# Attention and a two-layer network in one kernel: turning q and k of nineteen quads on TensorE instead of by a transposing DMA

## The chip, the core and the metric

The kernel runs on one core of a Trainium2 chip. The metric is the device time of one execution, in microseconds (us). A core has a matrix engine (TensorE, PE in the profile; its weight loads are listed apart as PEld), VectorE (DVE), ScalarE (ACT), GpSimd (POOL) and a queue engine that only issues transfers (SyncE, SP). PSUM, where PE writes, has eight banks here, numbered 0 to 7. Each engine works through its own instructions in order.

## What is computed

```python
q, k, v                     # (8, 12, 448, 64): batch, heads, positions, head width
scores = scale * q @ k.T    # for each batch and head
attn   = maximum(scores, 0) ** 2 / 448
x      = attn @ v           # gathered to (3584, 768)
h      = x @ w_in           # (3584, 2048)
g      = maximum(h, 0) + alpha * minimum(h, 0)
out    = g @ w_out          # (3584, 768)
```

The score of a query and a key sums over the head width of 64, so PE needs q and k with the 64 columns of a head on the partitions and the positions along a row. They arrive the other way round, with positions on the partitions. "Turning" below means that step.

## The kernel before

**Tiling.** The 12 heads of a batch are taken four at a time, which gives 3 groups for each of 8 batches: 24 "quads", numbered 0 to 23. A quad has 7 chunks of keys. Matrix operands are bf16.

**The steps of a quad.** `load_qk` and `load_v` issue loads on POOL's queue into tiles of shape 128 x 896 (`raw`, three buffers each for q and k; `v`, six). q and k are turned into one tile `T` (four buffers). `score_mm` (L209) makes the scores of one chunk in a pair of PSUM banks, `relu` (L218 on ACT, L220 on DVE) and `square` (L231 on DVE, L229 on ACT) follow, and `attnv` (L241) multiplies with v over all 7 chunks and writes the quad's part of `xT`. When a batch has its three quads, `f1_mm` (L275) makes the first layer in 16 units of 6 matmuls, each followed by `f1_out` (L281 on ACT, then L282 on DVE); the second layer is either `f2` (L300) or a seven-product scheme (`Pair`, L335, with sums on DVE at L331 and L340).

**Two ways of turning.** Quads 0 to 4 go through `turn_pe` (L176 to L186). For each of q and k it takes a PSUM bank and issues 14 transposes on PE (7 position groups times 2 head halves, L183), each with 64 columns of the raw tile as weights and the 128-column identity streaming past; the two halves of a position group write partitions 0 to 63 and 64 to 127 of the bank. Then one copy (L186) brings the 128 x 896 bank to `T`. Quads 5 to 23 go through `turn_dma` (L188 to L199): two copies on ACT or DVE (L195) rearrange q and k into one tile (`perm`, a single buffer, or for quads 5, 7 and 8 a stretch of `w_mix`), and a transposing DMA on SP's queue (L197) writes `T`. After it, `land` (L418) makes POOL copy one element of `T`, so that POOL's queue stands still until the transfer has landed; the loads of later quads are issued behind it.

**What sets the order.** The order is written out by hand in the strings at L506 to L518, one word for each step, and each engine gets its instructions in that order. The words that matter here are `d6D` (turn quad 6, copies on DVE), `l6` (`land`), `n` (`prepare`: turn the next quad, then load q and k of the quad two further and v of the next), `c` (score chunks), `v` (`attnv`), `f`, `h`, `e`, `E` (first layer, in one go or in parts with a bank held) and `p1` to `p7`, `r1` to `r7` (second layer). `FIRST_PAIR`, `EACH`, `ONE_PAIR` and `LAST` are the plans of one batch each; `EACH` is run three times. The turn of a quad stands well ahead of its first chunk.

**Banks.** `take_bank` gives the bank that was taken longest ago; once `paired` is set it prefers the partner of the bank taken last. `take_pair` gives the pair of neighbours longest unused, `hold` withdraws a bank until it is given back. A matmul into a bank waits until the previous contents have been read.

Of the kernel before, what the change touches and what calls it, by code (L numbers as in the profile page):

```python
# [11 lines left out]
BF16 = mybir.dt.bfloat16  # L12
# [4 lines left out]
NJ = 7  # L17
# [3 lines left out]
def kernel(  # L21
# [10 lines left out]
    nc = tc.nc  # L32
    B, H, S, D = q.shape
# [11 lines left out]
    singles = ctx.enter_context(tc.tile_pool(name="singles", bufs=1))  # L45
    raw_pool = ctx.enter_context(tc.tile_pool(name="raw", bufs=3))
    v_pool = ctx.enter_context(tc.tile_pool(name="v", bufs=6))
    perm_pool = ctx.enter_context(tc.tile_pool(name="perm", bufs=1))
    T_pool = ctx.enter_context(tc.tile_pool(name="T", bufs=4))
    rl_pool = ctx.enter_context(tc.tile_pool(name="rl", bufs=6))  # L50
    at_pool = ctx.enter_context(tc.tile_pool(name="at", bufs=10))
# [11 lines left out]
    w_mix = [singles.tile([128, KH, NH], BF16, name=f"w_mix{i}") for i in range(4)]  # L63
# [3 lines left out]
    landed = singles.tile([1, 1], BF16)  # L67
# [17 lines left out]
    def hold():  # L85
        i = one()
        taken[i] = 10**9
        return i
# [14 lines left out]
    def take_bank():  # L103
        i = one()
        take(i, 1)
        return psum[:, i]


    raw, vraw = {}, {}

    def load_qk(n, names="qk"):
        b, g = divmod(n, NG)
        for name in names:
            src = q if name == "q" else k
            t = raw_pool.tile([128, 2, NJ, D], BF16, tag=name, name=f"{name}raw")
            flat = src[b].rearrange("(m two) (pp j) d -> (two pp) m (j d)", two=2, j=NJ)
            nc.gpsimd.dma_start(out=t.rearrange("p m j d -> p m (j d)"), in_=flat[:, 2 * g:2 * g + 2])
            raw[(n, name)] = t

    def load_v(n):  # L120
        b, g = divmod(n, NG)
        t = v_pool.tile([128, 2, NJ, D], BF16, tag="v", name="vraw")
        flat = v[b].rearrange("(m two) (pp j) d -> (two pp) m (j d)", two=2, j=NJ)
        nc.gpsimd.dma_start(out=t.rearrange("p m j d -> p m (j d)"), in_=flat[:, 2 * g:2 * g + 2])
        vraw[n] = t
# [28 lines left out]
    for lo, hi, eng in ((0, 4, nc.sync), (4, NJ, nc.scalar)):  # L154
        t = o_pool.tile([128, 2, (hi - lo) * D], F32, tag="o", name=f"qfirst{lo}")
# [18 lines left out]
    T = {}  # L174

    def turn_pe(n, parts=(("q", 0, NJ, "D"), ("k", 0, NJ, "D"))):  # L176
        if n not in T:
            T[n] = T_pool.tile([128, 2, NJ, 128], BF16, tag="T", name="T")
        for name, lo, hi, eng in parts:
            ps = take_bank().bitcast(BF16)  # L180
            for j in range(lo, hi):
                for s in range(2):
                    nc.tensor.transpose(ps[64 * s:64 * s + 64, 128 * j:128 * j + 128], raw[(n, name)][:, s, j], ident)  # L183
            dst = T[n][:, "qk".index(name), lo:hi].rearrange("p j c -> p (j c)")
            copy = nc.vector.tensor_copy if eng == "D" else nc.scalar.copy
            copy(dst, ps[:, 128 * lo:128 * hi])  # L186

    def turn_dma(n, eng="A"):  # L188
        if n in (5, 7, 8):
            w = w_mix[2 + n % 2].rearrange("p k c -> p (k c)")[:, :4 * NJ * D]  # L190
            p = w.rearrange("p (a j s d) -> p a j s d", a=2, j=NJ, s=2)
        else:
            p = perm_pool.tile([128, 2, NJ, 2, D], BF16, tag="perm", name="perm")
        for i, name in enumerate("qk"):
            (nc.vector.tensor_copy if eng == "D" else nc.scalar.copy)(p[:, i], raw.pop((n, name)).rearrange("p s j d -> p j s d"))  # L195
        t = T_pool.tile([128, 2, NJ, 128], BF16, tag="T", name="T")
        nc.sync.dma_start_transpose(out=t.rearrange("p a j c -> p (a j) c"),  # L197
                                    in_=p.rearrange("p a j s d -> p (a j s d)"))
        T[n] = t  # L199


    att, xT = {}, {}
# [58 lines left out]
    def chunk(eng):  # L261
        if stream:
            n, j = stream.pop(0)
            late.append((n, j, relu(score_mm(n, j), eng)))

    def sq(i, eng):
        if i < len(late):
            square(*late.pop(i), eng)
# [4 lines left out]
    def f1_mm(ps, b, ff, ks):  # L273
        for km in ks:
            nc.tensor.matmul(ps, w_in_sb[:, km // 2, km % 2, bass.ts(ff, 128)],  # L275
                             xT[b][:, km // 2, km % 2, :],
                             start=(km == 0), stop=(km == KM - 1))

    def f1_out(ps, b, ff):
        neg = neg_pool.tile([128, S], F32, tag="neg", name="neg")  # L280
        nc.scalar.activation(neg, ps, ACTF.Relu, scale=-1.0)  # L281
        nc.vector.scalar_tensor_tensor(gT[:, ff, (b % 2) * S:(b % 2) * S + S],  # L282
                                       neg, beta_sb[:, ff:ff + 1], ps, ALU.mult, ALU.add)
# [121 lines left out]
        copy = nc.vector.tensor_copy if eng == "D" else nc.scalar.copy  # L405
        copy(raw[(0, "q")][:, :, lo:hi].rearrange("p m j d -> p m (j d)"), qfirst[lo][:, :, :D * (hi - lo)])

    def prepare(n, eng="A"):
        if n < NQ:
            turn_dma(n, eng)  # L410
            land(n)
        if n + 2 < NQ:
            load_qk(n + 2)
        if n + 1 < NQ:
            load_v(n + 1)

    def land(n):
        nc.gpsimd.tensor_copy(landed, T[n][:1, 0, 0, :1])  # L418

    class Walk:  # L420

# [11 lines left out]
        def step(self, w):  # L433
            c, rest = w[0], w[1:]
            if c == "c":
                for eng in rest:
                    chunk(eng)
            elif c == "s":
                sq(int(rest[:-1] or 0), rest[-1])
            elif c == "v":  # L440
                if turn["v"] < NQ:
                    attnv(turn["v"], rest or "AD")
                    turn["v"] += 1
            elif c == "f":
                b, ff, ps, _ = self.unit(self.b, self.ff)
                f1_mm(ps, b, ff, range(KM))
                f1_out(ps, b, ff)
            elif c == "m":
                self.open = self.unit(self.b, self.ff)
                f1_mm(self.open[2], *self.open[:2], range(KM))  # L450
            elif c == "o":
                f1_out(self.open[2], *self.open[:2])
            elif c == "e":
                for i in range(self.parts, self.parts + int(rest)):
                    ff, km = divmod(i, 4)
                    if km == 0:
                        self.held.append(self.unit(self.b, self.ff, hold()))
                    f1_mm(self.held[ff][2], self.b, ff, (km,))
                self.parts += int(rest)
            elif c == "h":  # L460
                self.held.append(self.unit(self.b, self.ff, hold()))
                f1_mm(self.held[-1][2], *self.held[-1][:2], range(4))
            elif c == "E":
                b, ff, ps, bank = self.held.pop(0)
                f1_mm(ps, b, ff, range(4, KM))
                f1_out(ps, b, ff)
                take(bank, 1)
            elif c == "B":
                self.b, self.ff = self.b + 1, 0
            elif c in "pr":  # L470
                if rest[0] in "abcd":
                    getattr(self, c).mix("abcd".index(rest[0]) + 1)
                else:
                    getattr(getattr(self, c), "p" + rest)()
            elif c == "w":
                i, half = int(rest[0]), int(rest[1])
                weight_mix(i, 4 * half, 4 * half + 4)
            elif c == "g":
                f2(self.b // 2, int(rest[0]), int(rest[1]))
            elif c == "n":  # L480
                prepare(self.quad, rest or "A")
                self.quad += 1
            elif c == "x":
                cast0(int(rest[0]), int(rest[1]), rest[2])
            elif c == "t":
                turn_pe(int(rest[0]), ((rest[1], int(rest[2]), int(rest[3]), rest[4]),))
            elif c == "d":
                turn_dma(int(rest[:-1]), rest[-1])
            elif c == "l":
                land(int(rest))  # L490
            elif c == "L":
                n = [int(x) for x in rest[1:].split(",")]
                {"q": load_qk, "v": load_v, "i": load_w_in, "o": load_w_out}[rest[0]](*n)
            elif c == "i":
                warm(int(rest))
            elif c == "y":
                bank = min(range(8), key=lambda i: (taken[i], i))
                for _ in range(int(rest)):
                    nc.tensor.matmul(psum[:, bank, :128], idle, idle, start=True, stop=True)
            elif c == "z":  # L500
                two_queues.append(1)
            elif c == "b":
                nc.vector.tensor_scalar(beta_sb, alpha_sb, -1.0, 1.0, ALU.mult, ALU.add)
# [48 lines left out]
```

## Time and profile before

| | us |
|---|---|
| median of the runs (372.81 to 373.34) | 373.07 |
| the profiled execution, whole time | 373.07 |
| its span, first to last instruction | 371.3 |
| outside the span | 1.8 |
| score matmuls, L209, 672, busy | 45.9 |
| attention-times-v matmuls, L241, 672, busy | 36.6 |
| first layer, L275, 768, busy | 150.4 |
| relu on ACT, L218, 128, busy | 111.2 |
| gate on DVE, L282, 128, busy | 85.3 |

The granted TensorE clock is 1.000 of full speed over the span. The slices of the profile have PE at 9 tenths or more from the third slice to the last but one, DVE and ACT between 4 and 9 for most of the span, and the 16 DMA engines at 8 or 9 tenths for the first 13 slices (about 120 us), then between 8 and 0. "Busy" is the time in which an engine has an instruction in flight; matmuls overlap each other, so the busy times of groups of matmuls are unions and not sums. The chain of waits follows the work that ended last back to the start; its rows are start, duration, engine, line and number of instructions.

### The profile page before, as it was taken

How to read it: one execution, taken by the hardware profiler on the slowest of the kernel's cores; microseconds unless marked ns; L12 is line 12 of the kernel's file. 1: busy time of each engine (PE TensorE's matmuls, PEld its weight loads, DVE VectorE, ACT ScalarE, POOL GpSimd, SP SyncE). 2: the span in 40 equal slices, each digit the busy share in tenths (PEclk: the TensorE clock that was granted, in tenths of full speed). 3: DMA queues.
4: the chain of work that ended last, by engine and by line, in shares of the span. 5: the costliest groups of instructions: out<-in, count | busy, mean ns of one | idle time of the engine just before them, and what ended most of it. 6: DMA issues, size and time to landing. Idle time of an engine off the chain costs nothing.

```text
span 371.3 us, 7894 instructions
## 1 busy us (share of the span) xinstructions
PE 363.6 (98%) x3105; PEld 197.5 (53%) x3105; DVE 278.0 (75%) x445; ACT 274.7 (74%) x406; POOL 71.7 (19%) x120
## 2 busy tenths in 40 slices
PE   8799999999999999999999999999999999999995
PEld 6454564444554565545555455554555455555563
DVE  3989988885968989566887768888749667856653
ACT  5998676877997678885997859967699866964400
POOL 8566150304211222022020220202200000000000
PEclk9999999999999999999999999999999999999999
DMA  9999989999999868455882659727646201220024
GB/s 143 188 203 202 199 135 191 153 160 167 180 171 150 123 96 163 92 89 90 160 144 64 99 80 168 144 56 121 111 89 134 49 2 43 65 65 0 0 64 108
DMA packets 73557, 43.29 MB, mean 117 GB/s; under 512 B 40368, under 2 KB 73008, under 8 KB 73520
## 3 DMA queue, kind: packets, MB, share of 16 engines
q0 software_dynamic: 27136, 22.58, 42.0%
q1 hardware_dynamic: 45712, 19.61, 25.9%
q10 hardware_dynamic: 672, 0.59, 0.5%
q8 instruction: 24, 0.39, 0.4%
q14 instruction: 13, 0.11, 0.1%
HBM read 45.62 MB, written 11.01 MB: 153 GB/s over the span
## 4 chain that ended last, share of the span: by engine, by line
PE 94%; DVE 2%; ACT 2%; issue 1%; ACTq 0%
PE psum L275 38%; PE psum L335 30%; PE psum L241 9%; PE psum L209 9%; PE psum L300 6%; PE psum L183 1%; PE psum L165 1%; DVE gT L282 1%; ACT rl L218 1%; ACT xT L253 1%; ACT neg L281 1%; DVE w_mix L195 1%; DVE T L186 0%; DVE at L231 0%; DVE osb L340 0%
## 5 line engine op out<-in xcount | busy, mean ns | idle before, releaser
L275 PE MATMUL psum<-xT,w_in_sb 128*128 128x448 bf16 x768 | 150.4, 353 | 0.2 <-DVE gT L282 0.2
L282 DVE SCALAR_TENSOR_TENSOR gT<-neg,beta_sb,psum 128x448 bf16<-128x448 f32 x128 | 85.3, 679 | 43.4 <-ACT neg L281 42.1
L218 ACT ACTIVATE rl<-psum 128x896 bf16<-128x896 f32 x128 | 111.2, 925 | 6.7 <-PE psum L209 4.7
L275 PEld LDWEIGHTS <-w_in_sb 128*128 128x128 bf16 x768 | 73.4, 98 | 73.0 <-issue 6.8
L281 ACT ACTIVATE neg<-psum 128x448 f32<-128x448 f32 x128 | 68.5, 547 | 41.0 <-PE psum L275 32.7
L231 DVE TENSOR_TENSOR at<-rl 128x896 bf16<-128x896 bf16 x105 | 62.2, 620 | 0.5 <-ACT rl L218 0.2
L229 ACT ACTIVATE at<-rl 128x896 bf16<-128x896 bf16 x63 | 58.6, 952 | 0.3
L335 PEld LDWEIGHTS <-S 128*128 128x128 bf16 x384 | 36.7, 98 | 28.4 <-issue 5.3
L335 PE MATMUL psum<-w_mix,S 128*128 128x384 bf16 x288 | 49.8, 326 | 0.2
L220 DVE TENSOR_SCALAR rl<-psum 128x896 bf16<-128x896 f32 x40 | 43.2, 1086 | 8.7 <-PE psum L209 8.1
L209 PE MATMUL psum<-T 64*64 64x448 bf16 x672 | 45.9, 357 | 2.0 <-DVE T L186 1.0
L418 POOL COPY landed<-T 1x1 bf16<-1x1 bf16 x18 | 3.3, 181 | 206.1 <-DMA T<-perm 182.9
L335 PEld LDWEIGHTS <-gT 128*128 128x128 bf16 x296 | 28.3, 98 | 20.2 <-issue 1.8
L241 PE MATMUL psum<-at,vraw 64*64 64x448 bf16 x672 | 36.6, 350 | 0.0
L335 PE MATMUL psum<-w_out_sb,gT 128*128 128x384 bf16 x192 | 34.0, 326 | 0.0
L340 DVE TENSOR_TENSOR osb<-psum,u 128x384 f32<-128x384 f32 (+2 forms) x37 | 20.2, 547 | 12.6 <-PE psum L335 8.2
L209 PEld LDWEIGHTS <-T 64*64 64x64 bf16 x672 | 17.4, 105 | 22.7 <-issue 14.8
L241 PEld LDWEIGHTS <-vraw 64*64 64x64 bf16 x672 | 21.2, 106 | 11.9 <-issue 2.9
L300 PE MATMUL psum<-w_out_sb,gT 128*128 128x256 bf16 (+1 forms) x128 | 22.0, 326 | 0.1
L255 DVE TENSOR_SCALAR xT<-psum 128x448 bf16<-128x448 f32 x24 | 14.9, 622 | 8.9 <-PE psum L241 8.3
L253 ACT ACTIVATE xT<-psum 128x448 bf16<-128x448 f32 x24 | 13.3, 556 | 9.1 <-PE psum L241 8.7
L356 ACT COPY osb<-psum 128x384 f32<-128x384 f32 x12 | 5.8, 480 | 17.4 <-PE psum L335 17.4
(45 smaller groups left out, 242.0 us busy)
## 6 DMA issues: line engine op xcount, KB each, us to landing
out_dram<-osb SPq DMA_DIRECT2D x91, 96.0 KB, 2.2
vraw<-in_v_dram POOLq DMA_DIRECT2D x24, 224.0 KB, 6.5
qraw<-in_q_dram POOLq DMA_DIRECT2D x23, 224.0 KB, 4.1
kraw<-in_k_dram POOLq DMA_DIRECT2D x23, 224.0 KB, 5.3
w_in_sb<-in_moe_w_in_dram POOLq DMA_DIRECT2D x16, 192.0 KB, 8.0
w_out_sb<-in_moe_w_out_dram POOLq DMA_DIRECT2D x4, 512.0 KB, 9.5
w_out_sb<-in_moe_w_out_dram POOLq DMA_DIRECT2D x4, 256.0 KB, 8.8
out_dram<-osb SPq DMA_DIRECT2D x8, 128.0 KB, 3.2
```

Of the source, the lines that this page charges most:

```text
L209: nc.tensor.matmul(ps[64 * c:64 * c + 64, r, :S], t[64 * r:64 * r + 64, 1, j, 64 * c:64 * c + 64], t[64 * r:64 * r + 64, 0, :, 64 * c:64 * ...
L218: nc.scalar.activation(rl, ps[:, :, :S], ACTF.Relu)
L220: nc.vector.tensor_scalar(rl, ps[:, :, :S], 0.0, None, ALU.max)
L229: nc.scalar.activation(a, rl, ACTF.Square)
L231: nc.vector.tensor_tensor(a, rl, rl, ALU.mult)
L241: nc.tensor.matmul(ps[64 * s:64 * s + 64, r, :S], vv[64 * r:64 * r + 64, s, j, :], a[64 * r:64 * r + 64, s], start=(j == 0), stop=(j == NJ ...
L275: nc.tensor.matmul(ps, w_in_sb[:, km // 2, km % 2, bass.ts(ff, 128)], xT[b][:, km // 2, km % 2, :], start=(km == 0), stop=(km == KM - 1))
L281: nc.scalar.activation(neg, ps, ACTF.Relu, scale=-1.0)
L282: nc.vector.scalar_tensor_tensor(gT[:, ff, (b % 2) * S:(b % 2) * S + S], neg, beta_sb[:, ff:ff + 1], ps, ALU.mult, ALU.add)
L300: nc.tensor.matmul(ps, gT[:, ff, bass.ts(c, 128)], w_out_sb[:, ff, first_col + lo:first_col + hi], start=(ff == 0), stop=(ff == KF - 1))
L335: nc.tensor.matmul(ps, left[:, i], right[:, i], start=(start and i == 0), stop=(i == KH - 1), skip_group_check=not start)
L340: nc.vector.tensor_tensor(t, ps, u, ALU.add)
```

## The change

Quads 5 to 23 are turned by `turn_pe` as well, through a new `turn_late`: q's bank is copied to `T` by ACT, k's by DVE, whatever engine the word of the plan names. `turn_dma`, the `perm` tile, the transposing DMA and `land` are no longer used; the words of the plan stay where they are.

```diff
-    perm_pool = ctx.enter_context(tc.tile_pool(name="perm", bufs=1))
...
-    def turn_dma(n, eng="A"):
-        if n in (5, 7, 8):
-            w = w_mix[2 + n % 2].rearrange("p k c -> p (k c)")[:, :4 * NJ * D]
-            p = w.rearrange("p (a j s d) -> p a j s d", a=2, j=NJ, s=2)
-        else:
-            p = perm_pool.tile([128, 2, NJ, 2, D], BF16, tag="perm", name="perm")
-        for i, name in enumerate("qk"):
-            (nc.vector.tensor_copy if eng == "D" else nc.scalar.copy)(p[:, i], raw.pop((n, name)).rearrange("p s j d -> p j s d"))
-        t = T_pool.tile([128, 2, NJ, 128], BF16, tag="T", name="T")
-        nc.sync.dma_start_transpose(out=t.rearrange("p a j c -> p (a j) c"),
-                                    in_=p.rearrange("p a j s d -> p (a j s d)"))
-        T[n] = t
+    def turn_late(n):
+        turn_pe(n, (("q", 0, NJ, "A"), ("k", 0, NJ, "D")))
...
-    def prepare(n, eng="A"):
+    def prepare(n):
         if n < NQ:
-            turn_dma(n, eng)
-            land(n)
+            turn_late(n)
         if n + 2 < NQ:
             load_qk(n + 2)
         if n + 1 < NQ:
             load_v(n + 1)
-
-    def land(n):
-        nc.gpsimd.tensor_copy(landed, T[n][:1, 0, 0, :1])
...
             elif c == "n":
-                prepare(self.quad, rest or "A")
+                prepare(self.quad)
...
             elif c == "d":
-                turn_dma(int(rest[:-1]), rest[-1])
+                turn_late(int(rest[:-1]))
             elif c == "l":
-                land(int(rest))
+                pass
```

## The prediction

> **What bounds the kernel now.** I read the page's busy times first, then what PE waits for, then the chain of waits.
>
> ```profile
> PE 363.6 (98%) x3105; PEld 197.5 (53%) x3105; DVE 278.0 (75%) x445; ACT 274.7 (74%) x406; POOL 71.7 (19%) x120
> ```
>
> A busy PE need not be a full one, so 98% proves little alone. The view of waits, limited to PE and to the stretch from 20 to 349 us, has a single row (total us, times, longest):
>
> ```profile
> PE psum L275 <- DVE gT L282: 0.2, 1, 0.2
> ```
>
> So in 329 us PE was seen waiting for 0.2 us. Of its 7.7 us of idle time 3.5 lie in the first 20 us and 3.7 after 349 us, where the change touches nothing; the rest are gaps too short to be listed. To see whether PE streams or only looks busy I take rates from the chain (start, us, what):
>
> ```profile
> 24.19 1.45 PE psum L241 x28
> 25.64 0.90 PE psum L183 x28
> 26.54 3.89 PE psum L275 x20
> ...
> 34.20 1.24 PE psum L275 x6
> 35.44 0.90 PE psum L183 x28
> 36.34 3.51 PE psum L275 x18
> ...
> 109.25 9.19 PE psum L275 x48
> ...
> 286.50 9.19 PE psum L275 x48
> ```
>
> 48 first-layer matmuls take 9.19 us at 109 us and at 286 us, 191.5 ns each, and those after the turns of quads 3 and 4 take 194.5 and 195. PE runs at one rate everywhere: it is the bound, and whatever is added to its queue between 20 and 349 us lengthens the span one for one.
>
> The same rows price the change: the 28 transposes (L183) of quad 3, and those of quad 4, take 0.90 us of the chain. Quad 3's follow L241 and quad 4's stand between first-layer matmuls, the two kinds of place that the new ones get.
>
> **What the change adds on PE.** Six turns (quads 5 to 10) are `d` words and thirteen (11 to 23) are `n` words, 19 in all, each with 28 transposes: 532 instructions. 19 x 0.90 = 17.1 us. Bounds: in the start-up the chain has 0.51 us for 14 transposes alone, so 14 more cost 0.90 - 0.51 = 0.39 and each excursion has a fixed part of 0.51 - 0.39 = 0.12. If a neighbour shared the fixed part a turn would cost 2 x 0.39 = 0.78, in all 14.8; if each bank paid its own, 2 x 0.51 = 1.02, in all 19.4. I take 0.90, since two whole quads in both kinds of place show exactly that.
>
> A rule speaks for a dearer price. The Trainium skill (TensorE: Matmul & The Clock Gate, section "Back-to-back issue gap") gives about 81 ns for each matmul of 128 columns in a sustained stream of weight load and matmul. By it, as an estimate, a quad would cost 28 x 81 ns = 2.27 us, the change 43 us, and the time would be 416. The chain's 0.90 us is 32 ns for each transpose; here the two head halves use different columns of the array, and the measured row decides.
>
> **What it removes and moves on ACT and DVE.** These are the groups of instructions, shapes kept apart (number, then busy us and mean ns, then idle before):
>
> ```profile
> L195 ACT COPY perm<-kraw 128x896 bf16<-128x896 bf16 x11 | 10.5, 957 | 0.0
> L195 ACT COPY perm<-qraw 128x896 bf16<-128x896 bf16 x11 | 10.4, 947 | 0.0
> ...
> L195 DVE COPY perm<-qraw 128x896 bf16<-128x896 bf16 x5 | 3.1, 612 | 0.0
> L195 DVE COPY perm<-kraw 128x896 bf16<-128x896 bf16 x5 | 3.0, 609 | 0.0
> ...
> L186 DVE COPY T<-psum 128x896 bf16<-128x896 bf16 x5 | 3.1, 622 | 0.2 <-PE psum L183 0.2
> ...
> L186 ACT COPY T<-psum 128x896 bf16<-128x896 bf16 x2 | 1.8, 922 | 0.0
> ```
>
> ACT loses 20.9 us (11 quads) and gains 19 x 0.922 = 17.5: 3.4 less. DVE loses 6.1 and another 3.6 for the three quads staged in `w_mix` (six copies of 0.61), and gains 19 x 0.622 = 11.8: 2.1 more. Both are about three quarters busy over a span that grows by 17, so neither becomes the bound on average. Where the turn is an `n` or a `d` word for ACT, ACT's share of the turn falls from 1.90 to 0.92; at the `D` words it gains 0.92 and DVE falls from 1.22 to 0.62. I cost this at nothing, covered by PE's own stream; without that cover it costs what the bank waits below cost.
>
> The one stage where another engine is nearly as late as PE is 60 to 71 us: DVE is busy 10.06 of 11.00 us and the chain runs through L281, L282 and L195. There quads 6, 7 and 8 are turned, and the 0.2 us wait above lies at its end. If DVE were the bound there, three turns (2.7 us) would hide. But PE's 44 first-layer matmuls from 60.45 to 68.88 us take 191.6 ns each, the full rate, so nothing hides; at most the 0.2 goes, since DVE loses 3 x 0.6.
>
> **What it removes on the queues.** 19 transposing DMAs leave SP's queue and 18 `landed` copies leave POOL's:
>
> ```profile
> POOL landed L418 <- DMA T<-perm: 182.9, 16, 19.4
> ...
> POOL landed L418 <- DMA T<-w_mix: 23.2, 2, 12.7
> ```
>
> These 206 us are POOL's, off the chain: nobody is seen waiting for POOL between 20 and 349 us. Their value is zero. What it triggers: loads of later quads are issued earlier, held back only by a free `raw` buffer.
>
> **The added waits.** PE now waits for the raw loads, where ACT or DVE did, and behind a waiting transpose stands everything on PE. Before, q and k of quad 12 were issued at 109.97 and 110.68 us and copied at 122.31, the shortest lead that I find from quad 11 on; the longest landing of a q or k load is 9.8 us. That fits before, and `land` no longer delays it. I take zero; if it failed at one quad by a whole landing it would cost up to 9.8 us. The consumer's side eases: the quickest use is quad 6, whose `T` landed at 66.5 us for scores at 68.88; the copies now follow the transposes within about 2 us.
>
> Each turn also takes two more banks. I followed the take counters through the plans. Most banks come round after more than 1.8 us of PE work, as before. Six places are tighter: quads 5, 9 (q and k) and 21 take a bank whose last matmul lies 0.69 to 1.14 us of PE work back, and in quads 16 and 19 `p5` takes q's bank after 0.45 us of k's transposes and 0.69 us of scores, 1.14 us. ACT's copy needs 0.92 and starts within 0.05 of the last transpose at quad 3 (last one ends at 26.15, copy starts 26.19), so 0.97 fits into 1.14 with an idle ACT; with one relu (0.925) ahead it is late by 0.75. Before, gaps of 0.69 occur at a dozen places and PE waited at none. Bounds: 0, and 6 x 0.75 = 4.5 us. I take 0, nearest to the rows.
>
> **The sum.** Own time 373.07 (span 371.3 and 1.8 around it; the median is the same 373.07). 373.07 + 17.1 = 390.2.
>
> **The rivals.**
>
> *PE has room after all (not slower).* The weight loads fill only 53%, and a half-width transpose could slip in beside a neighbour. Then the turns cost nothing, and the time is 373.07 less whatever the L195 copies put on the chain (1.14 + 1.05 us near 64 and 69 us): 370.9 to 373.1. A rule points this way: the Trainium skill (Perfetto Trace Analysis, section "Identifying the Most-Contended Engine") tells to judge TensorE by its weight-load share rather than by matmul occupancy, which here would leave nearly half free. It decides from 0.9 us of open PE time at each turn, 17 in all; the waits have 0.2 and the rate is level. Chance 2%.
>
> *A little room.* If each turn were eased by 0.2 us or more, through fewer collisions in PSUM or SBUF without the transposes' 8.7 MB (19 tiles of 128 x 1792 bf16) or ACT's 3.4 us, the time would be 386.4 or less, down to some 382. Against it: matmul rates are the same at 109 us, where DMA is busy, and at 286 us, where it is mostly not. Chance 7%.
>
> *Banks become the bound.* If every turn found ACT one relu behind, 19 x 0.75 = 14.3 us come on top: 404.5. Against it: 0.69 us gaps did no harm. Chance 9% for more than 394.7.
>
> *The halves do not overlap.* At the 110 ns median of an L183 weight load, 28 in a row take 3.1 us and the time is 373.07 + 58.5 = 431.6. The 0.90 speaks against it. Chance 2%.
>
> **How the numbers follow.** 80% for the forecast, 390.2. Its range reaches down to 373.07 + 14.8 - 0.2, about 387.6, and up to 390.2 + 4.5 = 394.7; both rivals next to it lie outside, so 20% is left out. About 2% (7.5 us) can be told from no change here: faster means under 365.6, slower over 380.5. Only the first rival ends below 380.5: 2% same, 1% faster for what I haven't thought of, 97% slower.
>
> **What would show it.** Right: 672 matmuls in L183 (140 + 532), L195, L197 and L418 gone, L183 on the chain with about 22 us in place of 1% of the span, 0.90 for each late quad, PE busy near 380.7, first-layer matmuls still 191.5 ns, ACT's total some 3 us lower and DVE's 2 higher. Wrong: PE waits on ACT or DVE copies at L186, or on raw loads; turns that take 1.5 us and more; or L275, L335 slower or faster than before.

## The result and the profile after

| | before | after |
|---|---|---|
| median of the runs, us | 373.07 | 395.23 |
| span of the profiled execution, us | 371.3 | 393.2 |

The ratio is 1.0594, with a 95% interval from 1.0548 to 1.0639: 22.2 us more, where 17.1 had been forecast, and 0.5 us above the upper end of the range. The line numbers shift in the changed kernel: the transposes are L182, their copies L185, the scores L198, relu on DVE L209, attention times v L230, the first layer L264, its gate L271, `f2` L289, the seven-product scheme L324 and the loads of q and k L116.

The busy times, and PE's waits between 20 and 372 us (total us, times, longest; before, this view had one row of 0.2 us):

```profile
PE 382.0 (97%) x3634; PEld 211.8 (54%) x3637; DVE 281.5 (72%) x448; ACT 273.4 (70%) x403; POOL 68.4 (17%) x102
```

```profile
PE psum L324 <- DVE xT L244: 0.9, 1, 0.9
PE psum L182 <- DMA kraw<-in_k_dram: 0.6, 1, 0.6
PE psum L182 <- DVE rl L209: 0.4, 1, 0.4
PE psum L289 <- DVE rl L209: 0.4, 1, 0.4
PE psum L182 <- DMA qraw<-in_q_dram: 0.2, 1, 0.2
```

PE is 18.4 us busier (363.6 before) and now waits at five places, 2.5 us in all. The chain of waits (start, us, what), at quad 5 and at quads 13, 14 and 16:

```profile
33.67 8.26 DMA kraw<-in_k_dram
41.98 0.58 PE psum L182 x14
42.56 4.65 PE psum L264 x24
...
146.95 0.90 PE psum L182 x28
...
164.21 3.51 PE psum L264 x18
167.72 0.90 PE psum L182 x28
168.62 5.78 PE psum L264 x30
...
195.22 0.90 PE psum L182 x28
196.12 0.69 PE psum L198 x12
```

The forecast 0.90 us stands in every row of an undisturbed turn (`x28`). But look at the run that quad 14's turn cuts. Before, these 48 first-layer matmuls were one piece:

```profile
152.57 9.19 PE psum L275 x48
```

Now they take 3.51 + 5.78 = 9.29 us. The turn costs 1.00 us, 0.10 of it in the row after its own. Laying the two chains side by side at the same piece of work (named by its line before the change) gives the whole account:

| turns | the piece compared | starts before and after, us | added by these turns, us |
|---|---|---|---|
| 5 | L275 x24 | 40.55, 42.56 | 2.0 |
| 6 to 8 | L335 x16 | 77.57, 82.18 | 2.6 |
| 9 | L209 x12 | 93.01, 99.00 | 1.4 |
| 10 | L209 x12 | 105.13, 113.12 | 2.0 |
| 11, 12 | L209 x12 | 132.21, 142.84 | 2.6 |
| 13 | L275 run | 152.57, 164.21 | 1.0 |
| 14 | L335 x8 | 167.09, 179.74 | 1.0 |
| 15 | L335 x8 | 170.66, 184.32 | 1.0 |
| 16 | L275 run | 198.52, 213.08 | 0.9 |
| 17, 18 | L335 x8 | 216.61, 233.19 | 2.0 |
| 19 | L275 run | 244.47, 261.95 | 0.9 |
| 20, 21 | L300 x16 | 263.53, 283.26 | 2.3 |
| 22, 23 | L275 x96 | 331.09, 352.84 | 2.0 |

The last difference is 21.75 us; the spans differ by 21.9. Undisturbed turns cost 1.0, and 0.9 at quads 16 and 19, which stand between L324 and L198. Quads 5, 6, 9 and 21 also stand between work of two shapes (64 x 64, as scores are, on one side and 128 x 128 on the other), and the experiments below show why 0.9 is the price there too. 13 x 1.01 + 6 x 0.90 is 18.5. The rows of quads 5, 9, 10, 12 and 21 hold 3.5 us more, where the waits are. The row of quads 6 to 8 holds 0.3 less: the one wait before, for VectorE, is gone, and the 36 first-layer matmuls around it take 6.92 us where they took 7.24 (69.57 to 76.81).

VectorE's part in the longest wait is in the timeline at quad 10 (start, us, engine, line; in brackets idle time before and its releaser):

```profile
103.81 1.09 DVE L209 TENSOR_SCALAR rl<-psum 128x896 bf16<-128x896 f32 x1 [0.22 <-PE psum L198]
...
105.35 1.82 DVE L302 TENSOR_TENSOR w_mix<-w_out_sb,w_mix 128x1536 bf16<-128x1536 bf16 x2
...
107.08 0.62 DVE L244 TENSOR_SCALAR xT<-psum 128x448 bf16<-128x448 f32 x1
...
107.76 4.06 PE L324 MATMUL psum<-w_mix,S 128*128 128x384 bf16 x24 [0.92 <-DVE xT L244]
```

Two weight sums of VectorE (L302) stand ahead of the eviction L244, and PE's next product wants the bank that L244 empties. Before, by the take counters in the code, the rotation gave that product a bank of earlier scores that ACT had read. At quad 5 the two timelines differ in who meets the load, DVE before the change and PE after it:

```profile
33.54 0.71 POOL L117 DMA_DIRECT2D kraw<-in_k_dram  x1 [0.42 <-PE psum L275]
...
42.14 0.61 DVE L195 COPY w_mix<-qraw 128x896 bf16<-128x896 bf16 x1
42.67 0.61 DVE L195 COPY w_mix<-kraw 128x896 bf16<-128x896 bf16 x1
```

```profile
40.78 0.58 PE L182 MATMUL psum<-ident,qraw 128*64 128x128 bf16 x14 [0.21 <-DMA qraw<-in_q_dram]
...
41.98 0.58 PE L182 MATMUL psum<-ident,kraw 128*64 128x128 bf16 x14 [0.61 <-DMA kraw<-in_k_dram]
```

DVE reached its copies at 42.1 us, after the load; PE comes to the same word of the plan at 40.6 and stands.

### The profile page after: what moved, and what is told of

It is laid out like the page before. It is cut to its first block, busy times and chain, and to the rows that moved or that the text cites. A ratio compares the mean times of both kernels' runs of the same rounds, so it can differ in the third digit from the quotient of the medians.

```text
span 393.2 us, 8842 instructions
## 1 busy us (share of the span) xinstructions
PE 382.0 (97%) x3634; PEld 211.8 (54%) x3637; DVE 281.5 (72%) x448; ACT 273.4 (70%) x403; POOL 68.4 (17%) x102
## 4 chain that ended last, share of the span: by engine, by line
PE 89%; DVE 4%; DMA 3%; ACT 1%; issue 1%; DVEq 0%; POOLq 0%
PE psum L264 36%; PE psum L324 28%; PE psum L230 8%; PE psum L198 7%; PE psum L289 5%; PE psum L182 4%; DMA kraw<-in_k_dram 3%; DVE rl L209 2%; DVE at L220 1%; DVE T L185 1%; ACT xT L242 1%; DVE gT L271 0%; DVE xT L244 0%; ACT neg L270 0%; DVE w_mix L302 0%
## 5 line engine op out<-in xcount | busy, mean ns | idle before, releaser
L264 PE MATMUL psum<-xT,w_in_sb 128*128 128x448 bf16 x768 | 151.5, 353 | 0.0
L271 DVE SCALAR_TENSOR_TENSOR gT<-neg,beta_sb,psum 128x448 bf16<-128x448 f32 x128 | 86.0, 679 | 55.4 <-ACT neg L270 54.9
L264 PEld LDWEIGHTS <-w_in_sb 128*128 128x128 bf16 x768 | 72.7, 98 | 71.2 <-issue 5.3
L324 PEld LDWEIGHTS <-S 128*128 128x128 bf16 x384 | 36.7, 98 | 29.2 <-issue 6.2
L324 PE MATMUL psum<-w_mix,S 128*128 128x384 bf16 x288 | 50.0, 326 | 1.2 <-DVE xT L244 0.9
L209 DVE TENSOR_SCALAR rl<-psum 128x896 bf16<-128x896 f32 x40 | 43.2, 1086 | 8.5 <-PE psum L198 8.3
L116 POOL DMA_DIRECT2D qraw<-in_q_dram x23 | 16.5, 718 | 184.3 <-PE psum L182 180.6
L198 PE MATMUL psum<-T 64*64 64x448 bf16 x672 | 45.6, 356 | 1.5 <-ACT rl L207 1.0
L324 PEld LDWEIGHTS <-gT 128*128 128x128 bf16 x296 | 28.1, 98 | 20.0 <-issue 1.8
L230 PE MATMUL psum<-at,vraw 64*64 64x448 bf16 x672 | 36.5, 350 | 0.0
L324 PE MATMUL psum<-w_out_sb,gT 128*128 128x384 bf16 x192 | 34.0, 326 | 0.0
L329 DVE TENSOR_TENSOR osb<-psum,u 128x384 f32<-128x384 f32 (+2 forms) x37 | 20.2, 546 | 13.5 <-PE psum L324 8.4
L198 PEld LDWEIGHTS <-T 64*64 64x64 bf16 x672 | 17.2, 105 | 21.5 <-issue 14.5
L230 PEld LDWEIGHTS <-vraw 64*64 64x64 bf16 x672 | 21.2, 106 | 11.9 <-issue 3.0
L185 ACT COPY T<-psum 128x896 bf16<-128x896 bf16 (+2 forms) x25 | 20.4, 820 | 4.7 <-PE psum L182 4.6
L289 PE MATMUL psum<-w_out_sb,gT 128*128 128x256 bf16 (+1 forms) x125 | 21.8, 325 | 0.6 <-DVE rl L209 0.4
L244 DVE TENSOR_SCALAR xT<-psum 128x448 bf16<-128x448 f32 x24 | 14.9, 622 | 9.2 <-PE psum L230 8.6
L185 DVE COPY T<-psum 128x896 bf16<-128x896 bf16 (+4 forms) x30 | 16.7, 560 | 4.1 <-PE psum L182 4.0
```

Source lines behind the costliest of these rows:

```text
L198: nc.tensor.matmul(ps[64 * c:64 * c + 64, r, :S], t[64 * r:64 * r + 64, 1, j, 64 * c:64 * c + 64], t[64 * r:64 * r + 64, 0, :, 64 * c:64 * ...
L209: nc.vector.tensor_scalar(rl, ps[:, :, :S], 0.0, None, ALU.max)
L230: nc.tensor.matmul(ps[64 * s:64 * s + 64, r, :S], vv[64 * r:64 * r + 64, s, j, :], a[64 * r:64 * r + 64, s], start=(j == 0), stop=(j == NJ ...
L289: nc.tensor.matmul(ps, gT[:, ff, bass.ts(c, 128)], w_out_sb[:, ff, first_col + lo:first_col + hi], start=(ff == 0), stop=(ff == KF - 1))
L324: nc.tensor.matmul(ps, left[:, i], right[:, i], start=(start and i == 0), stop=(i == KH - 1), skip_group_check=not start)
```

## The experiments

Four runs first, on one chip, beside which the kernel before ran at 373.21. All four start from the changed kernel (395.23).

**Quad 5's turn later.**

```diff
-... cAAA s0D s1D d5D f f s0D f l5 Lq6 ...
+... cAAA s0D s1D f f s0D f d5D l5 Lq6 ...
```

> Quad 5's turn stands behind three first-layer units more (about 3.5 us of PE work later). My theory: in the changed kernel PE reached this turn before k of quad 5 had landed and lost about 1.0 us there, once; so the time falls by 1.0 us, from 395.2 to 394.2, and no wait of L182 on a load is left. Rival: the transfers are simply late as a whole in this stage, and the next reader (the second layer's weights at 47 us) waits instead; then the time stays at 395.2.

394.26 us, 1.0 less than the changed kernel. The two waits on loads are gone from PE's list and the other three rows are as they were. The first theory holds: a load met too early, once, with nobody next in line.

**The crowded banks.**

```diff
-... cAA s1A d9A g11 w10 l9 s0D Lq11 Lv9 s0D cA w20 ...
+... cAA s1A g11 w10 l9 s0D Lq11 Lv9 s0D cA d9A w20 ...
-... s0D s1A w30 w31 vDA d10A l10 cA cA s3A p6 Lq12 ...
+... s0D s1A vDA d10A l10 cA cA s3A p6 w30 w31 Lq12 ...
-FIRST_PAIR ... s1A nD pa pb r1 f pc ...
+FIRST_PAIR ... s1A pa pb r1 f nD pc ...
-ONE_PAIR ... s1D cA s0D n s0D f f ...
+ONE_PAIR ... s1D cA s0D s0D f n f ...
```

> At quads 9, 12 and 21 the turn stands one step later, and two weight sums of VectorE stand behind p6 instead of ahead of the eviction that frees p6's bank. My theory: the two more banks that each turn takes let a matmul meet a bank that VectorE has not read yet, at quads 9, 10, 12 and 21, for 0.4, 1.0, 0.6 and 0.2 us; so the time falls by 2.2 us to 393.0, and PE's list of waits from 80 us on is empty. Rival: VectorE is the bound in this stage and the same microseconds come back at the next bank; then it falls by less than 0.7, to 394.5 or more.

393.38 us, 1.85 less, between the two. PE's waits, in the same view:

```profile
PE psum L182 <- DMA kraw<-in_k_dram: 0.6, 1, 0.6
PE psum L324 <- DVE osb L329: 0.4, 1, 0.4
PE psum L324 <- DVE xT L244: 0.2, 1, 0.2
PE psum L182 <- DMA qraw<-in_q_dram: 0.2, 1, 0.2
```

The waits at quads 9, 12 and 21 are gone and quad 10's fell from 0.9 to 0.2. The moved weight sums came back as a new wait of 0.4 behind the next sums of VectorE (L329): the list from 80 us on is not empty, as the theory had it, and in that one place the rival is right as well. Side by side with the changed kernel, the chain gains 0.5 us at quads 9 and 10 (after the loss at the new wait), 0.6 at quad 12 and 0.2 at quad 21, 1.3 in all. Another 0.3 lies at quad 5, which the edit does not touch: its k landed a little earlier in this execution, and the first-layer matmuls behind its turn start at 42.18 us and not 42.49.

**Transposes of full width.**

```diff
+WIDE = 11
...
+            if n >= WIDE:
+                t = raw_pool.tile([128, NJ, 2, D], BF16, tag=name, name=f"{name}raw")
+                src_v = src[b].rearrange("(m two) (pp j) d -> (two pp) m j d", two=2, j=NJ)
+                for m in range(2):
+                    nc.gpsimd.dma_start(out=t[:, :, m], in_=src_v[:, 2 * g + m])
...
+                if n >= WIDE:
+                    nc.tensor.transpose(ps[:, 128 * j:128 * j + 128], raw[(n, name)][:, j].rearrange("p s d -> p (s d)"), ident)
+                    continue
```

> Quads 11 to 23 are turned in 128-column pieces, 14 transposes instead of 28, with q and k loaded so that the two heads of a position lie side by side. My theory: besides 0.39 us for each bank a turn pays a fixed 0.12 us for itself and 0.10 us for the run of full-width matmuls that it cuts in two, both for the change of the array's shape; without that change a turn costs 14 x 56 ns = 0.78 us. 11 turns that cut a run save 0.23 and two beside score chunks 0.12: 2.8 us in all, 392.4. Rival: the fixed part belongs to the transposes themselves; then the time stays at 395.2. If 128-column pieces cost the 81 ns of a sustained stream, a turn takes 1.13 us and the time rises by 1.5 to 2 us.

392.32 us, 2.9 less, for 2.8 expected. The agreement is in part luck: 0.4 of it lies at quad 5, whose turn the edit leaves alone (the matmuls behind it start at 42.11 us and not 42.49), so the edited turns gave 2.5. Three of them stand between work of two shapes and not two (quad 21 with 16 and 19), which makes the expected saving 10 x 0.23 + 3 x 0.12 = 2.7. The combined run below has the same edit, and its chain at quads 14 and 20 is undisturbed (first layer L275, the turn L190):

```profile
161.69 3.51 PE psum L275 x18
165.20 0.78 PE psum L190 x14
165.98 5.68 PE psum L275 x30
...
258.28 2.38 PE psum L275 x12
260.66 0.78 PE psum L190 x14
261.44 9.08 PE psum L275 x48
```

14 transposes take 0.78 us, 56 ns each, and the run after them starts at full rate: 9.08 us for 48 where a run behind another shape of work takes 9.19. Both fixed parts, 0.12 and 0.10, are gone with the change of shape. It is not the number of transposes that carries them, as the next run shows. The 81 ns that the prediction weighed do not occur here either; in the same section of the Trainium skill (TensorE: Matmul & The Clock Gate, "Back-to-back issue gap") the formula for a single gap, 2.5 ns and 128 columns at 2.4 GHz, gives 55.8 ns and agrees with the row.

**Every late transpose twice.**

```diff
-            for j in range(lo, hi):
+            for j in [j for j in range(lo, hi) for _ in range(2 if n >= 5 else 1)]:
```

> Every transpose of quads 5 to 23 is issued twice into the same place; banks, copies and loads are unchanged. My theory: only the 28 ns of each further transpose count and the fixed parts do not, 19 x 0.78 = 14.8 us, so 410.0, less up to 2 us where the longer turn covers a wait. Rival: a turn's cost is proportional to its transposes, 19 x 1.01 = 19.2 us, so 414.4.

407.43 us, 12.2 more. A turn's row of the chain, with 56 pieces:

```profile
173.06 1.68 PE psum L182 x56
174.75 5.78 PE psum L264 x30
```

1.68 is 0.90 + 0.78, so the second half pays no fixed part, as the theory has it; the rival's 414.4 is out. The sum 14.8 came short by 2.6, a little more than the 2 allowed: of PE's 2.5 us of waits only one of 0.6 us, on quad 5's q, is left. That a longer turn gives the banks time to be read is the likely reason, not a tested one, and 0.7 us of the 2.6 are not traced.

Three more runs, on another chip; the kernel before ran at 373.10.

**All three savings together**, quad 5 later, the crowded banks and full width:

> The edits of the first three runs together: quad 5's turn later, the turns of quads 9, 12 and 21 and two weight sums moved, quads 11 to 23 in 128-column pieces. My theory: the three causes are separate, so the savings add: 395.2 - 1.0 - 1.9 - 2.9 = 389.4. Rival: they share a cover, and the sum comes short by 1 us or more, 390.5 and above. Either way it stays above the kernel before, by 19 turns of 0.78 to 1.0 us.

390.25 us, 5.0 less than the changed kernel and 4.5% above the one before (interval 1.0435 to 1.0471). It is 0.85 short of the sum, between theory and rival. The rival's shared cover is quad 5's wait: the bank run and the full-width run had each gained 0.3 to 0.4 us there, and the first run gains all of it, so the sum counts some 0.7 us twice. Another 0.2 lies ahead of every edited step: the scores near 40 us start at 40.05 and not 39.82. The two waits of L335 that the bank edit left, 0.6 us, are there again and are the only ones on PE. What remains against the kernel before is in the main the transposing itself.

**Turns beside 64-wide work.**

```diff
-EACH ... f n f f f f s2A f s1D cAAA s1D ... p1 nD f f r1 ... pb cA vDA s1D ...
+EACH ... f f f f f s2A f s1D cAAA n s1D ... p1 f f r1 ... pb cA vDA nD s1D ...
```

> In the batches that run the plan EACH the first two turns stand right behind score chunks or attention times v, and no longer cut a run of first-layer matmuls: five turns (quads 14, 15, 17, 18, 23). My theory: each saves the 0.10 us with which a cut run starts again, 0.5 us in all: 394.7; a batch with three turns takes 0.2 us less than the 48.87 us of the changed kernel (164.21 to 213.08 us). Rival: a run's start costs nothing and the 0.11 us come from elsewhere; then a batch takes 48.87 us as now.

396.06 us, 0.8 more, and the batch takes 49.13 us (164.05 to 213.18): my theory fell. Quad 15's turn now stands between attention times v and scores:

```profile
190.00 1.32 PE psum L230 x28
191.32 0.90 PE psum L182 x28
192.22 0.50 PE psum L198 x8
```

The 8 score matmuls behind it take 0.50 where they took 0.38 behind L230. From the first `p1` of the batch to the product behind these scores (179.94 to 192.73 us) the piece takes 12.79 us, and 12.77 in the changed kernel (179.74 to 192.51): nothing is saved. So it is not the cut run of full-width matmuls that costs; each change between shapes (128 x 128, 64 x 64, the transposes' 128 x 64) costs 0.10 to 0.12 us in these rows, whichever of the two neighbours stands there. A turn put between two pieces of equal shape adds two changes, 0.78 + 0.23 = 1.01. At quads 16 and 19 the change from L324 to L198 was there already, so only one is added: 0.78 + 0.12 = 0.90. At quads 5, 9 and 21 a change was there already as well, and the run behind the turn takes what it took before (4.65 us for 24 matmuls, 3.61 for 16, 6.92 for 36); quad 6 stands between L230 and L264 in the same way. The Trainium skill (TensorEngine Tiling (Array Packing), section "Key Properties") says that changing the tiling mode drains TensorE. The rows here agree, with 0.10 to 0.12 us for a change; that a drain is what takes this time, no run shows. The rest of the loss is a bank again: quads 14, 17 and 23 wait 0.8 us together for L271.

**The kernel before without the wait for the transfer.**

```diff
     def land(n):
-        nc.gpsimd.tensor_copy(landed, T[n][:1, 0, 0, :1])
+        pass
```

> The kernel before without the one-element copies with which GpSimd waits for each transposing transfer; the loads behind them are issued earlier. My theory: nobody waits for these loads, so the time stays at 373.1. Rival: the earlier loads collide with the transposing transfers or with the weights, and T lands late somewhere: up to some us slower; or the loads were late for somebody, and it is faster.

383.45 us, 10.3 more than before (ratio 1.0271, interval 1.0245 to 1.0296): the rival, and larger than I had thought. PE's waits from 20 us on, and the chain:

```profile
PE psum L209 <- DMA T<-w_mix: 6.6, 2, 5.8
PE psum L209 <- DMA T<-perm: 0.5, 1, 0.5
```

```profile
43.75 15.35 DMA T<-w_mix
59.10 0.04 issue
59.14 1.33 PE psum L209 x11
60.48 2.61 PE psum L241 x25
...
71.04 3.19 DMA T<-perm
74.23 15.96 DMA T<-w_mix
90.19 0.04 issue
90.23 0.38 PE psum L209 x4
```

The transfer of quad 5 has the loads of quads 6 to 8 and the second layer's weights issued around it, those of quads 7 and 8 have q, k and v of later quads. These transfers take 15 to 16 us in the chain (the longest before was 12.0), and the scores stand. From 119 us on the chain runs as before, 9.8 us later throughout. `land` was no idle wait: it kept the loads off the transfers. In the changed kernel there is no such transfer to keep off, and PE waits for no load behind quad 5, so no cost of its removal shows there; but I had put its value at zero for the wrong reason. POOL still waits in the changed kernel, 180.6 us for the transposes (L182) that free a raw buffer.

## Why the prediction was wrong

- **PE is the bound and what is added to its queue adds to the span: right.** 18.4 us of busy time and 2.5 of waits make nearly the whole difference (21.9 in the span).
- **532 transposes at 0.90 us a turn: the row right, the term mis-sized.** The step was "I take 0.90, since two whole quads in both kinds of place show exactly that". A turn costs 0.78 and 0.10 to 0.12 for each change of shape that it adds: 1.01 at thirteen places, 0.90 at six. That is 18.5 and not 17.1, 1.4 us of the 5.1 missing. Quad 3's turn stood where one change was there already; quad 4's added two, and its second one was in the row behind. The prediction's own fence held it: 6 matmuls in 1.24 us, 18 in 3.51 and 48 in 9.19 are 189 ns each and 0.10 for the start of a run. I divided each row by its count, read 191.5 to 195 as one rate, and so put the start of the cut run nowhere. The upper bound of 1.02 had the size by luck, with another reason.
- **The load wait at zero: wrong by 1.1 us** (2.0 at quad 5, less 0.90 for the turn). I searched for the shortest lead "from quad 11 on". Quad 5's k was issued at 33.54 us and copied at 42.67 before, a lead of 9.1 against a longest landing of 9.8 that stood in the same paragraph. Moving the turn took the wait away again; the time fell by 1.0, since in its new place the turn adds one change of shape more.
- **The banks at zero: wrong by about 2.4 us, inside the bounds named (0 to 4.5):** 0.5 at quad 9, 1.0 at 10, 0.6 at 12, 0.3 at 21. The mechanism was the rival's, but not its engine: I priced ACT's copy one relu late, and it was VectorE that read late, behind evictions, weight sums and the gate. Of the six places listed, quads 5, 16 and 19 cost nothing by a bank and quad 21 some 0.3 us; quad 9's loss came one step later, and those at 10 and 12 were on banks with 1.4 to 2.1 us of PE work between uses, which my list leaves out or passes as safe. The edit that thinned the crowded banks gave back 1.3 us.
- **ACT 3 us less, DVE 2 more: 1.3 less and 3.5 more.** The old copies were issued in pairs that overlap (starts 0.83 us apart, 0.95 long, at 91.71 and 92.54), so a sum of durations overstated what was removed, by some 1.2 of ACT's 2.1 us; the rest is not traced. Neither engine became the bound, as said.
- **The queues at zero: right for this change**, with the reservation that the last run shows: `land` was worth 10.3 us in the kernel before.
- **The rivals.** Room on PE, a rate without overlap and the 81 ns are out by the 0.90 of every undisturbed turn. A little room (386.4 or less) is out too: the only easing seen is the 0.3 us at quads 6 to 8, where I had allowed 0.2. The full price for the banks (404.5) is out; a sixth of it occurred.
- **The account.** 1.4, 1.1 and 2.4, less 0.3, make 4.6 of the 5.1 us missing. The rest is the step from the chain's 21.75 to the 22.2 of the medians.

## What to carry to other kernels

On an engine that streams, price an added group of instructions by what the work around it takes with and without it, and not by the group's own row: fit duration against count over runs of several lengths, and the fixed part of each start shows; count the changes of shape that the group adds. When work moves from one engine to another, ask again who meets each load and each bank first; a lead that was safe for a lagging engine need not be for the one that runs ahead. A wait that nobody seems to wait for may be what holds transfers apart, so its price is known only once it has been taken out.

## What else the runs showed

In the last run PE stood 5.8 us before the scores near 59 us, and afterwards 25 matmuls of L241 took 2.61 us where 28 take 1.32. The same stretch by windows (us, length and PE busy, then the other engines; the third number from the end is PE's granted clock, then the DMA engines' share and GB/s):

```profile
55.00:57.00 2.00, 0.00 (x0) 0.00 (x0) 0.00 (x0) 0.00 (x0) 0.00 (x0) 1.00 1.22 197
57.00:59.00 2.00, 0.00 (x0) 0.00 (x0) 0.00 (x0) 0.00 (x0) 0.00 (x0) 0.59 1.23 207
59.00:61.00 2.00, 1.86 (x20) 0.92 (x24) 0.84 (x1) 1.22 (x2) 0.00 (x0) 0.50 1.21 242
61.00:63.00 2.00, 2.00 (x28) 1.03 (x24) 0.25 (x1) 0.51 (x1) 0.00 (x0) 0.50 1.26 236
63.00:65.00 2.00, 2.00 (x18) 0.71 (x11) 1.76 (x4) 1.88 (x3) 0.00 (x0) 0.70 1.22 200
```

PE stands from 53.3 us (59.1 less 5.8). A mean of 0.59 between 57 and 59 us fits a fall to one half at about 57.4 us, some four idle microseconds later, and a mean of 0.70 between 63 and 65 fits a return near 64 us; both times are estimates from these rows. PE's listed waits are 7.1 us, while the span grew by 9.8. Neither the kernel before nor the changed one pays this: from 20 us on PE's longest wait is 0.9 us, and the granted clock is 1.000 in both.

No experiment pointed to a version that beats the kernel before: each microsecond that came back was one that the change had cost.
